# Seven weight buffers at seven offsets modulo 256 bytes, in an attention and two dense blocks on one core

## The chip, the core and the metric

One NeuronCore of a Trainium2 chip runs one program. The metric is device time in microseconds, the median of several executions. Engines are named as in the profile: PE (TensorE's matrix products), PEld (TensorE's loads of the stationary operand), DVE, ACT, POOL and SP, whose queue issues the transfers.

## What is computed

Attention over 2 x 8 heads of 768 tokens and width 64, with a mask (a query sees only the keys of the same 6-bit hash), and two dense blocks on the 1536 token rows of width 512:

```python
scores = np.where(q_bucket[..., None] == k_bucket[..., None, :], q @ k.T / 8, -1e9)
x = softmax(scores) @ v                                   # 1536 x 512 after the heads are joined
h = np.maximum(np.maximum(x @ w1, x @ w2), x @ w3)        # 512 -> 768
x = h @ w_out                                             # 768 -> 512
h = x @ w_in                                              # 512 -> 2048
g = np.where(h >= 1, h, np.where(h <= -1, 0, (h + 1) ** 2 / 4))
out = g @ w_out2                                          # 2048 -> 512
```

## The kernel before

Every float is kept as a high and a low part in a reduced format, and a product is made of three (high x high, high x low, low x high; `mm3`, L704 to L711), all summed in one PSUM bank.

**Attention** (L249 to L699) runs first. Its order on the engines comes from a planner (`Work`, L42 to L107) with costs and due times. PE makes the scores (`t_qk`, L374 and L377), transposes the exponentials against `ident` (`t_tr`, L404) and multiplies them by the values (`g_pv`, L422); `bits_mm` (L337) makes the hash bits. The sums of the exponentials of two heads lie in a tile `sums` (L393).

**The dense layers** (`mlp`, L713 to L862) follow, each matrix product 128 rows by 512 columns (L708 or L835), with a load of its own for the stationary operand. Layer 1 (`l1`) runs over 18 slices of the weights and three blocks of 512 tokens, 12 products each: stationary is the weight slice, moving is `x_hl`. Six pieces of it are made ahead, in part at half width. Layer 2 (L786 to L799) has the weights stationary and `hh` moving. Layer 3 (`l3`) has the weights stationary and `x_hl` moving. Layer 4 (`l4`, L824) has it reversed: `g` is stationary and the weights move. From its third unit on, layer 3 alternates with layer 4 by groups of 12 products.

**The weights** come in 58 slices. `w_load` fetches one, `w_steps` (L182 to L215) decodes it in six steps on ACT and DVE, the last of which is a cast of the high part into its buffer (L213), and `w_low` (L217) makes the low part on POOL. Slice n goes to buffer n mod 7: five buffers `w` in the pool `w_p`, and two buffers `wx` in a pool that is opened when attention's tiles are gone. Slices are decoded ahead of their use, in ticks between the products.

**Where the tiles lie.** Pools are laid out one behind the other in each partition. The offset of a tile modulo 256 bytes, in the built programs:

| tile | role | before | after the change |
|---|---|---|---|
| `ident`, `x_hl`, `wr`, `wg`, `wg2` | identity; activations; decoding | 0 | 0 |
| `w`, five buffers | weights | 0 each | 0, 32, 64, 96, 128 |
| `wx`, two buffers | weights | 128 each | 160, 192 |
| `hh`, `acc`, `g`, the dense layers' `r` | layer 2's input; sums; layer 4's input | 128 | 224 |
| `h0` to `h2` | layer 1's maxima | 0 | 160 |
| `hi`, `lo`, `qa`, `qb`, `p`, `pt`, `vr`, attention's `r`, `u` and more | attention | 128 | 160 |
| `pj_st`, high and low | hash projection | 64 and 240 | 64 and 240 |

Inside these tiles, products start at multiples of 256 bytes: the parts and blocks of a weight buffer lie 2048 and 512 bytes apart. A seventh of the slices, then, falls on each buffer.

Of the kernel before, what the change touches and what calls it, by code (L numbers as in the profile page):

```python
# [8 lines left out]
F32 = mybir.dt.float32  # L9
F32R = mybir.dt.float32r  # L10
# [9 lines left out]
NK = S // 128  # L20
# [90 lines left out]
def lsh_attention_moe_kernel(  # L111
# [21 lines left out]
    w_p = ctx.enter_context(tc.tile_pool(name="w", bufs=1))  # L133
    t_p = ctx.enter_context(tc.tile_pool(name="t", bufs=1))
    nm_p = ctx.enter_context(tc.tile_pool(name="nm", bufs=2))
# [30 lines left out]
        slices += s3[:1] + s4 + s3[1:]  # L166
    key_index = {key: n for n, (key, _, _) in enumerate(slices)}
    NSL = len(slices)
    WEARLY, WBUFS = 5, 7
    raws, splits, low_todo = {}, {}, []  # L170
    w_state = {"raw": 0, "done": 0, "base": 0, "gen": None, "auto": False, "more": None}

    def w_load(upto):
        while w_state["raw"] < min(upto, NSL):
            n = w_state["raw"]
            _, src, cols = slices[n]
            r = w_p.tile([128, 512, 2], I32, tag="wr", name="wr", bufs=2)
            nc.sync.dma_start(out=r[:, 0:cols, :].rearrange("p c t -> p (c t)"), in_=src.bitcast(I32))
            raws[n] = r
            w_state["raw"] += 1  # L180

    def w_steps(n):  # L182
        w_load(n + 2)
        cols = slices[n][2]
        r = raws.pop(n)
        low, high = r[:, 0:cols, 0], r[:, 0:cols, 1]
        g = w_p.tile([128, 512], I32, tag="wg", name="wg", bufs=2)[:, 0:cols]
        if w_state["auto"]:
            w_low()
        nc.scalar.activation(out=f32(g), in_=f32(high), func=ACTF.Square)  # L190
        yield
        nc.vector.scalar_tensor_tensor(  # L192
            out=f32(g), in0=f32(g), scalar=TINY_SQ, in1=f32(high), op0=ALU.is_ge, op1=ALU.mult
        )
        yield
        g2 = w_p.tile([128, 512], I32, tag="wg2", name="wg2", bufs=2)[:, 0:cols]
        nc.vector.tensor_scalar(  # L197
            out=g2, in0=g, scalar1=3, scalar2=0x3FFFFFF8, op0=ALU.logical_shift_left, op1=ALU.bitwise_and
        )
        yield  # L200
        nc.vector.scalar_tensor_tensor(
            out=g2, in0=g, scalar=-0x40000000, in1=g2, op0=ALU.bitwise_and, op1=ALU.bitwise_or
        )
        yield
        nc.vector.scalar_tensor_tensor(  # L205
            out=g2, in0=low, scalar=29, in1=g2, op0=ALU.logical_shift_right, op1=ALU.bitwise_or
        )
        yield
        if n % WBUFS < WEARLY:
            w = w_p.tile([128, 2, 512], F32R, tag="w", name="w", bufs=WEARLY)  # L210
        else:
            w = w_state["more"].tile([128, 2, 512], F32R, tag="wx", name="wx", bufs=WBUFS - WEARLY)
        nc.scalar.copy(out=w[:, 0, 0:cols], in_=f32(g2))  # L213
        splits[n] = w
        low_todo.append((n, w, g2, cols))  # L215

    def w_low():  # L217
        for n, w, g2, cols in low_todo:
            nc.gpsimd.tensor_tensor(out=w[:, 1, 0:cols], in0=f32(g2), in1=f32(w[:, 0, 0:cols]), op=ALU.subtract)  # L219
        low_todo.clear()  # L220

    def w_tick(count=1):
        for _ in range(count):
            if w_state["gen"] is None:
                n = w_state["done"]
                if n >= NSL:
                    w_low()
                if n >= NSL or n >= w_state["base"] + (WBUFS if w_state["more"] else WEARLY):
                    return
                w_state["gen"] = w_steps(n)  # L230
            try:
                next(w_state["gen"])
            except StopIteration:
                w_state["gen"] = None
                w_state["done"] += 1
# [13 lines left out]
    def attention(mlp_steps):  # L249
        with ExitStack() as ax, ExitStack() as sx:  # L250
# [10 lines left out]
            head, pair, tl, grp = {}, {}, {}, {}  # L261
# [128 lines left out]
            def t_exp(n):  # L390
                h, t = divmod(n, NK)
                if n % (2 * NK) == 0:
                    pair[h // 2] = dict(sums=nm_p.tile([128, 2 * NK], F32, tag="sums", name="sums"))  # L393
                p = tl[n]["p"]
                c = (h % 2) * NK + t
                nc.scalar.activation(  # L396
                    out=p, in_=p, func=ACTF.Exp, scale=-1.0, bias=tl[n]["nm"],
                    accum_out=pair[h // 2]["sums"][:, c:c + 1],
                )
# [199 lines left out]
            def tile_tasks(n):  # L599
                h, t = divmod(n, NK)  # L600
                g, r = divmod(n, 3)
                sp, pp = place("s", 1), place("p", 2)
                tb = [place(f"t{i}", 1) for i in range(2)]
                if n % (2 * NK) == 0:
                    sums_p[h // 2] = place("sums", 1)
                if r == 0:
                    pt_p_[g] = place("pt", 1)
                qk = task("PE", 0.75, n, t_qk, n, after=ready[h], takes=[sp], leaves=[h_place[h]])
                mx = task("DVE", 0.97, n, t_max, n, after=[qk], takes=[pp], leaves=[sp])
                ex = task("ACT", 1.06, n, t_exp, n, after=[mx], takes=[sums_p[h // 2]] if n % (2 * NK) == 0 else [], lag=0.1)  # L610
                exps[n] = ex
                outs, tr = [], None
                for half in range(2):
                    tr = task("PE", 0.325, n - 4, t_tr, n, half, after=[ex, tr], takes=[tb[half]], leaves=[pp], lag=0.1)
                    cp = task("ACT", 0.48, n - 2, t_out, n, half, nc.scalar.copy, after=[tr], takes=[pt_p_[g]] if r == 0 and half == 0 else [], leaves=[tb[half]])
                    work.also("DVE", 0.55, lambda a=(n, half, nc.vector.tensor_copy): t_out(*a), cp)
                    outs += [cp]
                return outs
# [34 lines left out]
            for n in range(NT_):  # L653
                h, t = divmod(n, NK)
# [259 lines left out]
```

## Time and profile before

| | us |
|---|---|
| median of 3 runs (704.96 to 705.01) | 704.96 |
| profiled execution | 704.98 |
| its span, first to last instruction | 703.2 |
| PE busy (99% of the span) | 695.2 |
| DVE, ACT, POOL busy | 455.5, 374.0, 282.7 |
| PE waiting for another engine, in all | under 5 |

The profiled execution's own time is 1.78 us over its span. A timeline's row gives a group's start and its length; the length reaches to the end of the last product, which is pipelined with the next group, so that the pace of a group is the difference of two starts over the count.

### The profile page before, as it was taken

The numbers are of one execution on the slowest core, as the hardware profiler recorded it, in microseconds if no ns is written. First come the engines' busy times: TensorE is split into PE (matmuls) and PEld (weight loads), VectorE is DVE, ScalarE is ACT, GpSimd is POOL, SyncE is SP. The second block draws the span as 40 slices with busy tenths as digits, with TensorE's granted clock in tenths as the row PEclk, the third lists the DMA queues.
The fourth block names the chain that finished last, engine by engine and source line by source line (L and its number), as shares of the span: only waits on it lengthen the run. The fifth ranks groups of instructions, "written<-read, shape, count | busy, mean of one in ns | idle before, by whom it ended". The sixth has DMA issues, their size and how long they took to land.

```text
span 703.2 us, 9982 instructions
## 1 busy us (share of the span) xinstructions
PE 695.2 (99%) x3548; PEld 553.9 (79%) x3548; DVE 455.5 (65%) x696; ACT 374.0 (53%) x733; POOL 282.7 (40%) x262
## 2 busy tenths in 40 slices
PE   8999999999999999999999999999999999999998
PEld 6777777777777688888888888888888888888886
DVE  6646555666655486775444355765888888888844
ACT  4788898888888423332321233665544444444430
POOL 3555646647523034442332022444344344344330
PEclk9999999999999999999999999999999999999999
DMA  5655557546511222221111022120111122111004
GB/s 164 162 149 151 132 145 202 139 121 167 132 46 45 95 91 90 90 91 52 56 49 54 31 89 90 47 75 31 60 61 61 60 66 84 61 61 60 31 0 180
DMA packets 25658, 62.78 MB, mean 89 GB/s; under 512 B 4085, under 2 KB 9813, under 8 KB 25609
## 3 DMA queue, kind: packets, MB, share of 16 engines
q1 hardware_dynamic: 25576, 62.15, 29.2%
q8 instruction: 28, 0.46, 0.3%
q14 instruction: 22, 0.17, 0.1%
q0 software_dynamic: 32, 0.00, 0.0%
HBM read 42.07 MB, written 3.19 MB: 64 GB/s over the span
## 4 chain that ended last, share of the span: by engine, by line
PE 97%; DVE 1%; issue 0%; DMA 0%; ACT 0%; DVEq 0%; ACTq 0%
PE b L708 47%; PE b L835 19%; PE u_ps L422 10%; PE t_ps L404 9%; PE s_ps L374 5%; PE s_ps L377 5%; PE pj_ps L337 2%; DMA r<-in_kq 0%; DVE p L384 0%; DVE lo L302 0%; DVE qb L344 0%; DVE qa L331 0%; DVE pt L413 0%; PE pj_ps L469 0%; ACT pt L413 0%
## 5 line engine op out<-in xcount | busy, mean ns | idle before, releaser
L708 PE MATMUL b<-x_hl,w 128*128 128x512 f32 (+1 forms) x900 | 203.1, 382 | 0.0
L708 PEld LDWEIGHTS b<-x_hl,w 128*128 128x128 f32 x900 | 164.0, 188 | 34.2 <-issue 0.6
L384 DVE TENSOR_SCALAR_CACHE_REDUCE p<-s_ps 128x768 f32<-128x768 f32 x96 | 91.1, 955 | 43.7 <-PE s_ps L377 32.4
L735 POOL TENSOR_TENSOR g<-r,g 128x512 fp32r<-128x512 f32 x48 | 62.6, 1306 | 125.6 <-ACT g L734 125.6
L835 PE MATMUL b<-w,g 128*128 128x512 f32 (+1 forms) x438 | 108.4, 392 | 0.0
L219 POOL TENSOR_TENSOR w<-wg,w 128x512 fp32r<-128x512 f32 (+1 forms) x42 | 59.4, 1414 | 96.7 <-ACT w L213 80.8
L835 PEld LDWEIGHTS b<-w,g 128*128 128x128 f32 x438 | 81.9, 189 | 18.7
L396 ACT ACTIVATE p<-p,nm 128x768 f32<-128x768 f32 x96 | 89.8, 937 | 9.0 <-DVE p L384 8.5
L192 DVE SCALAR_TENSOR_TENSOR wg<-wg,wr 128x512 f32<-128x512 f32 (+1 forms) x58 | 66.1, 1140 | 36.2 <-ACT wg L190 35.4
L213 ACT CAST w<-wg 128x512 fp32r<-128x512 f32 (+1 forms) x42 | 25.4, 605 | 115.6 <-DVE wg L205 115.6
L708 PE MATMUL b<-x_hl,wx 128*128 128x512 f32 x360 | 86.1, 395 | 0.0
L404 PEld LDWEIGHTS t_ps<-ident,p 128*128 128x128 f32 x576 | 66.5, 140 | 22.7 <-ACT p L396 11.5
L404 PE MATMUL t_ps<-ident,p 128*128 128x128 f32 x576 | 82.1, 276 | 1.1 <-DVE pt L413 0.9
L708 PEld LDWEIGHTS b<-x_hl,wx 128*128 128x128 f32 x360 | 67.9, 189 | 15.8
L413 ACT COPY pt<-t_ps 128x384 f32<-128x384 f32 x158 | 69.5, 480 | 18.2 <-PE t_ps L404 16.3
L374 PE MATMUL s_ps<-lo,qa 128*128 128x384 f32 x192 | 72.3, 377 | 1.0 <-DVE p L384 0.9
L422 PE MATMUL u_ps<-pt,vr 128*64 128x384 f32 x384 | 69.6, 495 | 0.2 <-ACT pt L413 0.2
L377 PE MATMUL s_ps<-hi,qb 76*128 76x384 f32 x192 | 65.3, 340 | 0.2 <-DVE hi L331 0.2
L815 DVE SCALAR_TENSOR_TENSOR r<-r,b 128x512 f32<-128x512 f32 x48 | 33.0, 687 | 48.2 <-ACT r L814 47.8
L842 DVE TENSOR_TENSOR acc<-b,acc 128x512 f32<-128x512 f32 (+1 forms) x85 | 56.5, 676 | 8.0 <-PE b L835 8.0
L813 ACT ACTIVATE r<-b,half_sb 128x512 f32<-128x512 f32 x48 | 32.9, 686 | 46.1 <-PE b L708 40.8
L197 DVE TENSOR_SCALAR wg<-wg 128x512 int32<-128x512 int32 (+1 forms) x58 | 53.9, 929 | 2.8
(80 smaller groups left out, 847.5 us busy)
## 6 DMA issues: line engine op xcount, KB each, us to landing
wr<-in_w SPq DMA_DIRECT2D x50, 512.0 KB, 3.1
r<-in_kq SPq DMA_DIRECT2D x15, 384.0 KB, 3.9
vr<-in_v SPq DMA_DIRECT2D x16, 192.0 KB
rb<-d SPq DMA_DIRECT2D x16, 192.0 KB, 3.3
wr<-in_w SPq DMA_DIRECT2D x8, 384.0 KB, 2.8
qa<-hi SPq DMA_DIRECT2D x15, 192.0 KB
qb<-hi SPq DMA_DIRECT2D x15, 192.0 KB, 4.0
qa<-lo SPq DMA_DIRECT2D x15, 192.0 KB, 2.7
```

Source lines behind the costliest of these rows:

```text
L192: nc.vector.scalar_tensor_tensor(out=f32(g), in0=f32(g), scalar=TINY_SQ, in1=f32(high), op0=ALU.is_ge, op1=ALU.mult)
L219: nc.gpsimd.tensor_tensor(out=w[:, 1, 0:cols], in0=f32(g2), in1=f32(w[:, 0, 0:cols]), op=ALU.subtract)
L374: nc.tensor.matmul(out=o, lhsT=hd["qa"][:, qs], rhs=hd["lo"][:, ks], start=True, stop=False)
L377: nc.tensor.matmul(out=o, lhsT=hd["qb"][0:76, qs], rhs=hd["hi"][0:76, ks], start=False, stop=True)
L384: nc.vector.tensor_scalar(out=p.rearrange("p (a k) -> p a k", a=2), in0=s_ps[n % 2][:, :, 0:HALF], scalar1=MASKED, scalar2=MASKED, op0=ALU ...
L396: nc.scalar.activation(out=p, in_=p, func=ACTF.Exp, scale=-1.0, bias=tl[n]["nm"], accum_out=pair[h // 2]["sums"][:, c:c + 1],)
L404: nc.tensor.transpose(out=t_ps[half][:, j * 128:(j + 1) * 128], in_=tl[n]["p"][:, kt * 128:(kt + 1) * 128], identity=ident,)
L413: copy(out=grp[g][:, 3 * half:3 * half + 3, r * 128:(r + 1) * 128], in_=t_ps[half][:, 0:HALF].rearrange("p (j q) -> p j q", j=3),)
L422: nc.tensor.matmul(out=u_ps[rows, 0:HALF], lhsT=vr[:, kt, :], rhs=grp[g][:, kt, :], start=(i == 0), stop=(i == 2),)
L708: nc.tensor.matmul(out=outp, lhsT=w_[a], rhs=x_[b_], start=(i == 0 and jj == 0), stop=(i == n - 1 and jj == 2),)
L735: nc.gpsimd.tensor_tensor(out=dst[:, 1, cs], in0=src, in1=f32(dst[:, 0, cs]), op=ALU.subtract)
L835: nc.tensor.matmul(out=pb[:, cs], lhsT=gs[f][:, a, tsl], rhs=wt[:, b_, cs], start=(n == 0), stop=(n == len(terms) - 1),)
```

## The change

The weight tiles are 8 elements (32 bytes) longer per partition, and the part in use is cut from the front of each. In one pool the buffers thereby begin 4128 bytes apart in place of 4096. `sums` is padded from 48 to 256 bytes, of which the first 48 are used. All tiles behind the weights move. The instructions, their number and their order on every engine are the same; addresses alone differ.

```diff
-    WEARLY, WBUFS = 5, 7
+    WEARLY, WBUFS, STAG = 5, 7, 8
...
         if n % WBUFS < WEARLY:
-            w = w_p.tile([128, 2, 512], F32R, tag="w", name="w", bufs=WEARLY)
+            w = w_p.tile([128, 2 * 512 + STAG], F32R, tag="w", name="w", bufs=WEARLY)
         else:
-            w = w_state["more"].tile([128, 2, 512], F32R, tag="wx", name="wx", bufs=WBUFS - WEARLY)
+            w = w_state["more"].tile([128, 2 * 512 + STAG], F32R, tag="wx", name="wx", bufs=WBUFS - WEARLY)
+        w = w[:, 0:2 * 512].rearrange("p (a c) -> p a c", a=2)
         nc.scalar.copy(out=w[:, 0, 0:cols], in_=f32(g2))
...
                 if n % (2 * NK) == 0:
-                    pair[h // 2] = dict(sums=nm_p.tile([128, 2 * NK], F32, tag="sums", name="sums"))
+                    pair[h // 2] = dict(sums=nm_p.tile([128, 64], F32, tag="sums", name="sums")[:, 0:2 * NK])
```

## Rows read from the trace of the kernel before

**Rows 1.** The page: span, busy time by engine, granted clock in 40 slices.

```profile
span 703.2 us, 9982 instructions
...
PE 695.2 (99%) x3548; PEld 553.9 (79%) x3548; DVE 455.5 (65%) x696; ACT 374.0 (53%) x733; POOL 282.7 (40%) x262
...
PEclk9999999999999999999999999999999999999999
```

**Rows 2.** The waits of PE: releaser, us in total, times, longest.

```profile
PE t_ps L265 <- DVE warm L147: 1.1, 1, 1.1
...
PE s_ps L377 <- DVE hi L331: 0.2, 1, 0.2
```

**Rows 3.** Groups of PE's products by line and shape; moving operand first, then stationary.

```profile
L708 PE MATMUL b<-x_hl,w 128*128 128x512 f32 x828 | 195.3, 391 | 0.0
L835 PE MATMUL b<-w,g 128*128 128x512 f32 x426 | 107.0, 395 | 0.0
L708 PE MATMUL b<-x_hl,wx 128*128 128x512 f32 x360 | 86.1, 395 | 0.0
L404 PE MATMUL t_ps<-ident,p 128*128 128x128 f32 x576 | 82.1, 276 | 1.1 <-DVE pt L413 0.9 <-ACT pt L413 0.2
...
L708 PE MATMUL b<-hh,w 128*128 128x512 f32 x162 | 38.7, 395 | 0.0
L835 PE MATMUL b<-wx,g 128*128 128x512 f32 x144 | 37.9, 391 | 0.0
...
L337 PE MATMUL pj_ps<-hi,pj_st 128*108 128x384 f32 x62 | 17.1, 355 | 1.1 <-ACT pj_st L289 0.6 <-DVE pj_st L290 0.5
L708 PE MATMUL b<-hh,wx 128*128 128x512 f32 x54 | 13.2, 392 | 0.0
L337 PE MATMUL pj_ps<-lo,pj_st 128*108 128x384 f32 x31 | 10.4, 337 | 0.0
```

**Rows 4.** PE's timeline, layer 1: start us, length us, line, operands, count.

```profile
293.19 41.02 PE L708 MATMUL b<-x_hl,w 128*128 128x512 f32 x180
334.05 16.91 PE L708 MATMUL b<-x_hl,wx 128*128 128x512 f32 x72
350.80 32.85 PE L708 MATMUL b<-x_hl,w 128*128 128x512 f32 x144
383.48 2.25 PE L708 MATMUL b<-hh,w 128*128 128x512 f32 x9
```

**Rows 5.** PE's timeline, layer 2 and the start of layer 3.

```profile
404.31 2.21 PE L708 MATMUL b<-hh,wx 128*128 128x512 f32 x9
406.36 27.36 PE L708 MATMUL b<-hh,w 128*128 128x512 f32 x117
433.55 16.89 PE L708 MATMUL b<-x_hl,wx 128*128 128x512 f32 x72
```

**Rows 6.** PE's timeline, layers 3 and 4 in turn, at two places.

```profile
453.01 2.96 PE L835 MATMUL b<-w,g 128*128 128x512 f32 x12
455.81 2.92 PE L708 MATMUL b<-x_hl,w 128*128 128x512 f32 x12
458.57 2.96 PE L835 MATMUL b<-w,g 128*128 128x512 f32 x12
...
486.33 2.89 PE L835 MATMUL b<-wx,g 128*128 128x512 f32 x12
489.06 2.89 PE L708 MATMUL b<-x_hl,w 128*128 128x512 f32 x12
491.79 2.89 PE L835 MATMUL b<-wx,g 128*128 128x512 f32 x12
```

**Rows 7.** The chain that ended last, layers 3 and 4, first and last piece.

```profile
453.18 2.80 PE b L835 x12
...
680.32 19.55 PE b L835 x90
```

**Rows 8.** POOL's group that writes the low parts into `w`: busy us, mean ns.

```profile
L219 POOL TENSOR_TENSOR w<-wg,w 128x512 fp32r<-128x512 f32 x36 | 53.3, 1480 | 67.7 <-ACT w L213 58.1 <-issue 9.4
```

## Prediction

> **What bounds the kernel now.** I read the page's busy shares first. TensorE is busy for 695.2 of 703.2 us, no other engine for more than 455.5 [rows 1], and its granted clock reads 9, nine tenths or more, in all 40 slices [rows 1]: the upper of its two levels, 2.4 GHz. The list of what PE waited for names eight waits, from 1.1 us down to 0.2 [rows 2]. So the time is PE's own pace, and faster or slower work of ACT, DVE and POOL reaches the end only when PE would wait for it.
>
> Then the pace of the products of the dense layers, in PE's timeline, as the start of one group less the start of the one before it, divided by its count. All are 128 rows by 512 columns with a weight load each, 1974 of them (828 + 426 + 360 + 162 + 144 + 54) [rows 3]. The reader is to see that they have **two paces**, and what separates them:
> - Layer 1, stationary operand in `w` (offset 0), moving `x_hl` (offset 0): 293.19 to 334.05 holds 180, so 227.0 ns each; 350.80 to 383.48 holds 144, 226.9 ns [rows 4].
> - Layer 1, stationary in `wx` (offset 128), moving `x_hl` (0): 334.05 to 350.80 holds 72, 232.6 ns [rows 4]; four slices of the 18 are in `wx`.
> - Layer 2 has it the other way round: moving `hh` lies at 128. Stationary in `w` (0): 406.36 to 433.55 holds 117, 232.4 ns. Stationary in `wx` (128): 404.31 to 406.36 holds 9, 227.8 ns [rows 5].
> - Layers 3 and 4 alternate in twelves. Where `g` (128) multiplies `w` (0), a twelve takes 2.80 us and the layer 3 twelve after it, though both its operands lie at 0, takes 2.76 (453.01, 455.81, 458.57). Where `g` (128) multiplies `wx` (128), both kinds take 2.73 (486.33, 489.06, 491.79) [rows 6].
>
> So PE runs at 226.9 ns where the two operands have the same offset modulo 256, and at 232.4 where they are 128 apart, in either direction; one unequal group also costs its equal neighbour some 2.5 ns each. The engine, the line and the clock are the same, and PE waits for nobody there. The steady difference of 5.5 ns is 2.4% of the pace. This is what the change turns.
>
> **The change part by part.** The instructions and their order stay. What moves is addresses (the table of offsets above).
>
> *The dense layers.* After the change the stationary operand of layers 1 and 3 stands 0, 32, 64, 96, 128, 160 or 192 bytes ahead of `x_hl`, each in a seventh of the slices. Layer 2 (`hh` at 224) and layer 4 (`g` at 224) get 32 to 224 and never 0. The trace has only the distances 0 and 128 for these products, so the price of the six new ones is open. The sum now, by stages:
> - layer 1: 612 full products, 144 of them from `wx`: 468 x 227.0 + 144 x 232.6 ns = 139.7 us [rows 4];
> - layer 2: 383.48 to 433.55 = 50.1 us for 216 [rows 4, 5];
> - the first 84 of layer 3: 433.55 to 453.01 = 19.5 us [rows 5, 6];
> - the rest: 453.18 to 699.87 (680.32 + 19.55) [rows 7], 246.7 us, less 1.4 for twelve half-width ones (116 ns each, half the slow pace), 245.3 us for 1062.
>
> Together 454.6 us for 1974, 230.3 ns on average. So today's kernel is already nearer the slow pace: most of layers 2 to 4 is unequal. After the change a seventh of layers 1 and 3, 170 products (612 + 576 over 7), keeps distance 0: 38.6 us at 227.0. The other 1804 break even at (454.6 - 38.6) / 1804 = **230.6 ns**. Every ns off that is worth 1.80 us.
>
> What pace do they get? Bounds from both sides: 232.4 ns (all like 128) gives 1804 x 1.8 ns = +3.2 us; 226.9 (all like 0) gives -6.7 us. That a new distance is better than 0, or worse than 128, nothing in the trace excludes; one step of 5.5 ns beyond either (221.4, 237.9) would give -16.6 and +13.2 us, which I keep as the outer ends with little weight. I take the middle of the two measured paces, 229.7 ns, as the distances 32 to 224 lie on a circle on which 0 and 128 are opposite, three to each side: 1804 x (229.7 - 230.6) = **-1.6 us**. By stage, layer 1 loses (468 products leave 227.0 for an average near 229.3, 139.7 to 140.3 us, +0.6), layer 2 gains (216 x 229.7 = 49.6, -0.5), the 1146 of layers 3 and 4 gain (264.8 to some 263.1, -1.7).
>
> *Attention.* `p`, `hi`, `lo`, `qa`, `qb`, `pt` and `vr` all shift by the same 32 bytes, so `s_ps` and `u_ps` keep their distances. Two pairs change: the transposes (`p` against `ident`, 128 to 160, 576 of them) and the bit products (`pj_st` against `hi` and `lo`, 93) [rows 3]. The trace has each at its present distance alone, with no second pace to change to. I take both at nothing; the bounds are a whole step of 5.5 ns each way, 576 x 5.5 = 3.2 us and 93 x 5.5 = 0.5 us.
>
> *The other engines.* ACT's casts and POOL's subtractions (36 of 1480 ns into `w` [rows 8]) write to new offsets. In the dense layers PE sits idle for 0.0 us before its products [rows 3], and the eight waits of the whole run, under 5 us together [rows 2], lie before them; that slack covers them. If the cover were gone, POOL's step would be late first, by a few per cent of its 1480 ns. The padded sums cost 384 bytes a partition and no instruction.
>
> **Rule and row.** The rows show PE slowed by where its two own operands stand. The Trainium skill says otherwise: "TensorE: Matmul & The Clock Gate", Part 2, gives PE two independent read ports and holds that loading the next weights takes no read bandwidth from the running matmul, and "SBUF — State Buffer", who interferes with whom, that PE waits on nobody. By that rule the sum is 0 and the time 705.0; the trace speaks against it with 227.0 against 232.4 ns.
>
> **The rivals.**
> 1. *No net change* (703.6 to 706.4). Either losses in layer 1 meet gains in layers 2 to 4 (new distances at 229.8 to 231.4 on average), or the pace doesn't hang on the distance at all but on something that goes along with it here, such as which tile is read: 705.0. The skill's rule above is the second of these. For the first: break-even lies inside the two measured paces. Against the second: `w` is fast with `x_hl` and slow with `hh`, and `wx` the reverse [rows 4, 5].
> 2. *Slower, the equal pace is lost.* If 226.9 belongs to equal offsets alone and every other distance runs like 128, 1804 products take 232.4: +3.2 us, **708.2**. It decides where the mean of the new distances passes 231.4. For it: in layers 3 and 4 even equal twelves slow to 2.76 us beside unequal ones [rows 6], and after the change nearly every twelve has unequal neighbours. Against it: two distances don't make a rule for eight.
> 3. *Most new distances are as good as 0.* If only those near 128 are slow, the mean is near 228: 1804 x -2.6 = -4.7 us, **700.3**. For it: layers 2 to 4 are where the slow pace sits now. Against it: the same twelves beside unequal ones.
>
> **How the numbers follow.** The profiled execution took 704.98 us, 1.78 us around its span, 0.02 over the median 704.96 of the runs; 704.98 - 1.6 = **703.4 us**. About 0.2% (1.4 us) is what a measurement can tell from none; the new distances must average under 229.85 ns for a gain that shows. Chances: forecast (702 to 703.55) 0.28, rival 3 and better 0.15, so faster 0.43; rival 1 0.32 (0.25 balance, 0.07 no dependence); rival 2 and worse 0.25. The range from 700.0 (mean 227.9 ns) to 708.2 (mean 232.4) leaves out the outer ends and a slow change in the transposes, some 2 in 10.
>
> **What would show it.** In the profile after: TensorE's share and the waits as now; in layer 1's timeline runs of 36 products per weight buffer with up to seven paces in turn, the fifth (distance 128) at 232.4 and the first at 227.0; no stretch of 180 at 227.0 left; layers 3 and 4 in twelves of 2.72 to 2.80 without the long 2.80/2.76 series. Attention should end within 1 us of 234.9. The prediction is wrong if layer 1 lies at 232 throughout (rival 2), if the paces don't differ by buffer (no dependence), if a buffer runs over 233 or under 226, or if the transposes' pace moves.

## The result and the profile after

The change takes 708.57 us (median of 3 runs, 708.56 to 708.71) against 704.96 before: ratio 1.0052, 95% interval 1.0034 to 1.007. It is slower by 3.6 us, about half a per cent, where a gain of 1.6 us was forecast; the range ended at 708.2.

The page after, its span and PE's busy time, in answer to [rows 1]:

```profile
span 706.9 us, 9982 instructions
...
PE 699.1 (99%) x3548; PEld 553.5 (78%) x3548; DVE 454.8 (64%) x696; ACT 374.3 (53%) x733; POOL 283.0 (40%) x262
```

The span grew by 3.7 us and PE's busy time by 3.9, with the same 3548 products; the other engines' busy times moved by 0.7 us at most. PE has the same eight waits as the list behind [rows 2], one of them 0.2 us shorter. So the time is again in the pace of PE.

Layer 1 of the changed kernel by slice. Each stretch runs from the first product of a slice to that of the next and holds 36 starts (the count of 37 includes one product that reaches in from before); columns: the stretch, its length, PE busy and count, granted clock, the DMA engines' share and GB/s. In the built program the five `w` buffers are handed out in the order 0, 128, 96, 64, 32, the first and then the others from the back. So from top to bottom the stationary operand stands 0, 128, 96, 64, 32, 160 and 192 bytes ahead of `x_hl`:

```profile
294.00:302.19 8.19, 8.19 (x37) 1.00 0.29 105
302.19:310.56 8.37, 8.37 (x37) 1.00 0.20 71
310.56:318.98 8.42, 8.42 (x37) 1.00 0.19 62
318.98:327.38 8.40, 8.40 (x37) 1.00 0.20 62
327.38:335.78 8.40, 8.40 (x37) 1.00 0.16 47
335.78:344.18 8.40, 8.40 (x37) 1.00 0.17 49
344.18:352.43 8.25, 8.25 (x37) 1.00 0.15 48
```

Read it as a length over 36 products: 227.5 ns at distance 0, then 232.5 at 128, 233.9 at 96, 233.3 at 64, 233.3 at 32, 233.3 at 160 and 229.2 at 192. One distance of seven is about as fast as before. Five lie at the slow pace of before (232.4 ns in [rows 5], 232.6 in [rows 4]) or over it, one between. The clock is 1.00 in every line, so it is none of it. The sum of the seven is 58.43 us; the same seven slices took 57.61 before (293.19 to 350.80, [rows 4]).

PE's timeline at the borders of the stages, in answer to [rows 4] and [rows 5]:

```profile
385.81 2.27 PE L709 MATMUL b<-hh,w 128*128 128x512 f32 x9
...
436.08 16.82 PE L709 MATMUL b<-x_hl,wx 128*128 128x512 f32 x72
...
455.49 0.85 PE L836 MATMUL b<-w,g 128*128 128x512 f32 x3
```

And the chain that ended last, pieces of layers 3 and 4 and the last one, in answer to [rows 6] and [rows 7]:

```profile
235.15 220.50 PE b L709 x984
...
455.65 2.77 PE b L836 x12
458.42 2.74 PE b L709 x12
...
469.45 2.79 PE b L709 x12
472.25 2.79 PE b L836 x12
...
684.07 19.55 PE b L836 x90
```

In [rows 6] a twelve of layer 4 took 2.80 us and one of layer 3 2.76, or both 2.73. Now both kinds wander between 2.74 and 2.80, and most lie at 2.77 or over. By stages, with the kernel before taken from [rows 4 to 7] and the first long piece of its own chain:

```profile
234.89 218.28 PE b L708 x984
```

The last column is the first run of the next section (the padding alone, all dense tiles at 0), also less the kernel before.

| stage | before | change | difference | all tiles at 0 |
|---|---|---|---|---|
| attention, to the first product of layer 1 | 234.89 | 235.15 | +0.26 | +0.27 |
| layer 1 | 148.59 | 150.66 | +2.07 | -0.89 |
| layer 2 | 50.07 | 50.27 | +0.20 | -1.11 |
| layer 3 before layer 4 sets in | 19.46 | 19.41 | -0.05 | -0.42 |
| layers 3 and 4 | 246.69 | 247.97 | +1.28 | -4.53 |

The differences of the change sum to 3.76 us, those of the run at 0 to -6.68; the spans moved by 3.7 and -6.7.

### The profile page after: what moved, and what is told of

The parts are those of the page before. It is cut to its first block, busy times and chain, and to the rows that moved or that the text cites. A ratio compares the mean times of both kernels' runs of the same rounds, so it can differ in the third digit from the quotient of the medians.

```text
span 706.9 us, 9982 instructions
## 1 busy us (share of the span) xinstructions
PE 699.1 (99%) x3548; PEld 553.5 (78%) x3548; DVE 454.8 (64%) x696; ACT 374.3 (53%) x733; POOL 283.0 (40%) x262
## 4 chain that ended last, share of the span: by engine, by line
PE 97%; DVE 1%; issue 0%; DMA 0%; ACT 0%; DVEq 0%; ACTq 0%
PE b L709 47%; PE b L836 19%; PE u_ps L423 10%; PE t_ps L405 9%; PE s_ps L375 5%; PE s_ps L378 5%; PE pj_ps L338 2%; DMA r<-in_kq 0%; DVE p L385 0%; DVE lo L303 0%; DVE qb L345 0%; DVE qa L332 0%; DVE pt L414 0%; PE pj_ps L470 0%; ACT pt L414 0%
## 5 line engine op out<-in xcount | busy, mean ns | idle before, releaser
L709 PE MATMUL b<-x_hl,w 128*128 128x512 f32 (+1 forms) x900 | 206.4, 385 | 0.0
```

The source lines that it names most:

```text
L709: nc.tensor.matmul(out=outp, lhsT=w_[a], rhs=x_[b_], start=(i == 0 and jj == 0), stop=(i == n - 1 and jj == 2),)
```

## The experiments

**The padding alone.** The kernel before, and of the change only the padded `sums`. Its 256-byte tiles put everything behind the weights on 0 modulo 256: `wx`, `hh` and `g` as well as `w` and `x_hl`, and attention's tiles too.

```diff
-    ... sums=nm_p.tile([128, 2 * NK], F32, tag="sums", name="sums")
+    ... sums=nm_p.tile([128, 64], F32, tag="sums", name="sums")[:, 0:2 * NK]
```

> The kernel before with the sums padded to 256 bytes and no stagger: every dense tile (w, wx, x_hl, hh, g) then begins at the same offset modulo 256, 0. Theory A (PE's pace hangs on the distance of its two operands modulo 256, and only distance 0 gives the fast pace): all 1974 dense products at 227.0 ns in place of 230.3 on average, 454.6 to 448.1 us, so 698.5 us, and no stretch of 232 in layers 2 to 4. Rival B (weight buffers that share an offset slow each other, as one is written while another is read): nothing gained, 705 us, or up to 709 if wx now shares with w. Rival C (the change's loss came from moving the tiles behind the weights, by the padding): slower than 705, near 708.5.

Measured: 698.15 us against 705.02 for the kernel before on the same chip, ratio 0.9902 (0.9887 to 0.9917). The chain that ended last in this run:

```profile
235.16 215.86 PE b L708 x984
451.02 2.72 PE b L835 x12
453.75 2.72 PE b L708 x12
456.46 2.72 PE b L835 x12
674.06 19.12 PE b L835 x90
```

Its timeline, layers 1 and 2 and what follows:

```profile
276.78 16.48 PE L708 MATMUL b<-x_hl,wx 128*128 128x512 f32 x72
293.10 40.96 PE L708 MATMUL b<-x_hl,w 128*128 128x512 f32 x180
333.90 16.48 PE L708 MATMUL b<-x_hl,wx 128*128 128x512 f32 x72
...
382.86 2.20 PE L708 MATMUL b<-hh,w 128*128 128x512 f32 x9
...
405.30 26.68 PE L708 MATMUL b<-hh,w 128*128 128x512 f32 x117
431.82 16.48 PE L708 MATMUL b<-x_hl,wx 128*128 128x512 f32 x72
448.14 2.88 PE L708 MATMUL b<-x_hl,w 128*128 128x512 f32 x12
450.86 2.88 PE L835 MATMUL b<-w,g 128*128 128x512 f32 x12
```

`wx` with `x_hl` is as fast as `w` now (293.10 - 276.78 over 72 and 333.90 - 293.10 over 180 are both 226.7 ns), `hh` with `w` too (431.82 - 405.30 over 117 = 226.7), and the twelves of layers 3 and 4 take 2.72 us each (226.7 ns a product), with nothing lost where the two layers meet. Theory A holds to 0.4 us. Rival B falls: all seven buffers share one offset here while ACT and POOL write some and PE reads others. Rival C falls too: the same padding that the change has is worth -6.9 us when the stagger is left out. Attention didn't gain: `p` now stands at the offset of `ident`, and within their groups the transposes start 116.7 ns apart on average, as in the traces of before (distance 128), of the change (160) and of the next run (32). So what follows is shown for the dense products, not for the transposes.

**The stagger alone.**

```diff
 (the change)
-    ... sums=nm_p.tile([128, 64], F32, tag="sums", name="sums")[:, 0:2 * NK]
+    ... sums=nm_p.tile([128, 2 * NK], F32, tag="sums", name="sums")
```

> The stagger alone, sums not padded: w at 0, 32, 64, 96, 128 as in the change, wx at 32 and 64, hh and g at 96. Theory A: nearly every distance is unequal still, so the change's time, 708.6 us within 1, with the five w buffers of layer 1 at the paces of the change (229.2, 232.4, 234.6, 233.3, 233.3 ns) and the two wx buffers now like the second and third w buffer (232.4, 234.6) in place of 233.4 and 229.2; layer 2 fast only in slices whose buffer lies at 96. Rival C (padding is to blame): 705 us.

Measured: 709.24 us, ratio 1.0059 (1.0044 to 1.0074). The two `wx` buffers, now 32 and 64 bytes ahead, in layer 1 (columns as above):

```profile
335.94:344.34 8.40, 8.40 (x37) 1.00 0.17 49
344.34:352.74 8.40, 8.40 (x37) 1.00 0.16 47
```

That is 233.3 ns each, which is what the buffers at 32 and 64 took in the change (its fifth and fourth stretch above), and the five `w` buffers run as in the change (227.2 to 233.9 ns by the starts in the trace), so theory A holds here too. The 232.4 and 234.6 of the expectation came from taking the buffers in the order of their offsets, in which they are not handed out; the stretches at the second and third place are those at 128 and 96. The seventh buffer is slower than in the change (it was 229.2 at 192). In layer 2 the buffer at 96, the offset of `hh`, is the fastest as expected, but takes 229.4 ns beside unequal products (27 starts in the trace; the other four distances 232.1 to 233.7). The total is as expected. So the loss is the stagger's: it costs 10.4 us on the padded kernel (698.15 to 708.57) and 4.2 on the kernel before (705.02 to 709.24). The padding is worth 6.9 us without the stagger and 0.7 with it (709.24 to 708.57), as most distances are then unequal either way.

**One common place that is not 0.**

```diff
 (the padding alone)
-    warm = const.tile([128, CH], BF16, name="warm")
+    warm = const.tile([128, CH + 32], BF16, name="warm")[:, 0:CH]
```

> As the first run, with every tile from the identity on 64 bytes further, so that all operands of the dense products begin at 64 modulo 256. Theory A (distance alone counts): the time of the first run within 0.3 us, 698.5 us by the theory. Rival D (the place itself counts, tiles must begin at a multiple of 256 or 128): slower than the first run, up to 708 us if all products take 232.

Measured: 698.28 us, ratio 0.9903 (0.9887 to 0.992). From its chain:

```profile
235.19 215.82 PE b L708 x984
451.01 2.72 PE b L835 x12
```

The twelves take 2.72 us as in the first run. A common place at 64 costs no more than one at 0; the distance has a price.

**A stagger of 256 bytes.**

```diff
 (the change)
-    WEARLY, WBUFS, STAG = 5, 7, 8
+    WEARLY, WBUFS, STAG = 5, 7, 64
```

> The change with a stagger of 256 bytes in place of 32: every buffer begins at 0 modulo 256, but at 0, 256, 0, 256, 0 and so on modulo 512. Theory A with a period of 256 bytes: the time of the first run within 0.3 us, 698.5 us by the theory. If the period is 512 or more: three of seven buffers at some 232 ns, about 2.5 us per 460 products, 701 to 703 us. Rival B (buffers must not share an offset): 705 us or more.

Measured: 698.16 us, ratio 0.9902 (0.9887 to 0.9917). Seven different places whose distances are multiples of 256 cost nothing: 256 bytes is a period of it.

**Steps of 4 bytes.**

```diff
 (the stagger of 256 bytes)
-        w = w[:, 0:2 * 512].rearrange("p (a c) -> p a c", a=2)
+        s = n % WBUFS
+        w = w[:, s:s + 2 * 512].rearrange("p (a c) -> p a c", a=2)
```

> Every dense tile at 0 modulo 256 as in the first run, but the seven weight buffers are used from 0, 4, 8, 12, 16, 20 and 24 bytes on (each buffer 4352 bytes long). Theory A1 (the two operands must begin in the same 32 bytes of the 256): the first run's 698.2 us. Theory A2 (the same byte is needed): six of seven buffers at 231 to 235 ns as with the distances of 32 and more, 707 to 709 us. Theory A3 (the loss grows with the distance): layer 1 by buffer 226.7 ns at 0 and up step by step, about 701 us.

Measured: 708.07 us, ratio 1.0048 (1.0031 to 1.0064). Layer 1 by slice, from distance 0 to 24 (columns as above):

```profile
293.62:301.79 8.17, 8.17 (x37) 1.00 0.23 80
301.79:310.16 8.37, 8.37 (x37) 1.00 0.18 65
310.16:318.45 8.30, 8.30 (x37) 1.00 0.20 63
318.45:326.75 8.29, 8.29 (x37) 1.00 0.18 63
326.75:335.14 8.39, 8.39 (x37) 1.00 0.14 47
335.14:343.54 8.40, 8.40 (x37) 1.00 0.16 49
343.54:351.86 8.32, 8.32 (x37) 1.00 0.16 47
```

Over 36: 226.9 ns at 0, then 232.5 at 4 bytes, 230.5, 230.3, 233.1, 233.3 and 231.1. One element of distance costs nearly as much as 32 bytes (233.3 ns above). A1 (the same 32 bytes) falls, and so does A3, as the loss does not grow with the distance; A2 holds in its time and in four of the six buffers, the two at 230.5 and 230.3 lie just under its 231.

**Just below 256.**

```diff
 (the run before)
-        s = n % WBUFS
+        s = (0, 60, 56, 48, 52, 4, 8)[n % WBUFS]
```

> As the run before, with the seven buffers used from 0, 240, 224, 192, 208, 16 and 32 bytes modulo 256: the distances that the change has not, just below 256, with 192 and 32 once more. Theory A2: every buffer but the first at 231 to 235 ns, 707 to 709 us. Theory A1 or A3, read on both sides: 240 and 16 near 227, 32 at 232.4 and 192 at 229.2 ns in layer 1 as in the change, 224 between; 703 to 706 us. A pace under 226.7 in any buffer would mean that distance 0 is not the best.

Measured: 707.17 us, ratio 1.0033 (1.002 to 1.0046). Layer 1 by slice, distances 0, 240, 224, 192, 208, 16, 32:

```profile
293.67:301.86 8.18, 8.18 (x37) 1.00 0.29 93
301.86:310.02 8.17, 8.17 (x37) 1.00 0.25 82
310.02:318.42 8.39, 8.39 (x37) 1.00 0.18 62
318.42:326.66 8.24, 8.24 (x37) 1.00 0.18 64
326.66:335.01 8.36, 8.36 (x37) 1.00 0.12 47
335.01:343.42 8.40, 8.40 (x37) 1.00 0.15 49
343.42:351.81 8.40, 8.40 (x37) 1.00 0.16 47
```

Here 240 is as fast as 0 (8.17 us over 36, 226.9 ns), against A2; 224 (233.1), 208 (232.1) and 16 (233.3) are slow, 192 has its 229 and 32 its 233 again. So equal offsets are not the only fast pair, but 13 of the 15 unequal distances that layer 1 meets in these runs and the change cost from 3.4 to 7 ns each; 240 costs nothing and 192 some 2. None runs under 226.7.

Among unequal products a fast pair loses its pace. In layer 4 of the run with steps of 4 bytes, two buffers alternate by three products; there the single starts in the trace give 232.5 ns at distance 0 (105 products) and 232.6 at 240 (72), in the midst of the other distances (230.0 to 235.7).

**The hash projection at the same place.**

```diff
 (the padding alone)
-    pj_raw = const.tile([128, 108], F32, name="pj_raw")
-    pj_st = const.tile([128, 2, 108], F32R, name="pj_st")
+    pj_raw = const.tile([128, 160], F32, name="pj_raw")[:, 0:108]
+    pj_st = const.tile([128, 2, 128], F32R, name="pj_st")[:, :, 0:108]
...
-    warm = const.tile([128, CH], BF16, name="warm")
+    warm = const.tile([128, CH + 80], BF16, name="warm")[:, 0:CH]
```

> The first run with the hash projection's two parts moved from 64 and 240 to 0 modulo 256, the offset of hi and lo, so that attention's bit products have distance 0 too; identity and x_hl stay at 0. Theory A, if short products gain as the long ones: 93 products by up to 5 ns, 0.3 to 0.5 us less than the first run, 697.7 us. If runs of two or three products among others are too short to reach the fast pace: no change within 0.2 us.

Measured: 698.08 us, ratio 0.9903 (0.9888 to 0.9918), 0.07 us from the first run, which ran on another chip. No change: the 93 short products come in twos and threes and gain nothing that can be told.

**Which pair: a product's own, or the next load?** The stationary operand of a product is loaded while the product before it streams (in the trace of before, the load for a product of layers 2 to 4 begins 1 to 4 ns after the start of the product before and takes 188), so the distance could count in a product or across two.

```diff
 (the padding alone)
-    x_hl = x_p.tile([128, 2, 4, NT], F32R, name="x_hl")
+    x_hl = x_p.tile([128, 2, 4 * NT + 32], F32R, name="x_hl")[:, :, 0:4 * NT].rearrange("p a (k t) -> p a k t", k=4)
...
-    w = w_p.tile([128, 2, 512], F32R, tag="w", name="w", bufs=WEARLY)
+    w = w_p.tile([128, 2, 512 + 32], F32R, tag="w", name="w", bufs=WEARLY)
...
-    hh["t"] = h_p.tile([128, 6, 2, NT], F32R, name="hh")
+    hh["t"] = h_p.tile([128, 6, 2, NT + 32], F32R, name="hh")
...
-    gt = g_p.tile([128, 2, NT], F32R, tag="g", name="g", bufs=4)
+    gt = g_p.tile([128, 2, NT + 32], F32R, tag="g", name="g", bufs=4)
```

(`wx` as `w`.)

> The first run with the low parts (of w, wx, x_hl, hh and g) 128 bytes further than the high parts, which stay at 0. In a triple (high x high, high x low, low x high) the two operands of one product are then 128 apart in the second and the third product; but the stationary operand that is loaded for the NEXT product always has the offset of the moving operand of the product that runs (0 and 0, 128 and 128, 0 and 0). Theory N (the load ahead meets the running stream, so the next product's stationary counts): no unequal pair, near the first run, 226.7 to 229 ns, 698.2 to 702 us. Theory O (a product's own two operands count): two of three products unequal, 230.5 to 232.5 ns, 705.5 to 709.5 us.

Measured: 706.63 us, ratio 1.0025 (1.0015 to 1.0035). In its timeline `x_hl` with `wx` and with `w` take the same:

```profile
277.01 16.80 PE L708 MATMUL b<-x_hl,wx 128*128 128x512 f32 x72
293.65 41.76 PE L708 MATMUL b<-x_hl,w 128*128 128x512 f32 x180
```

That is 16.64 us over 72, 231.1 ns, or 693.3 ns for a triple in place of 680.0. The number lies where theory O put it, but the run doesn't prove it: the place of the streams changes twice in every triple, and such a change has a price even where each product's own pair is equal. [Rows 6] show that: beside `wx` all products of both layers had equal operands, layer 3 at 0 and layer 4 at 128, and a twelve took 2.73 us; here above, with one place for all, 2.72. The single starts in the trace show that these 10 ns fall on the border: the last product of such a twelve takes 233 ns and the first of the next 230, those in between 226 or 227. Theory N alone, without such a price, falls. Which of the two pairs counts stays open.

## Why the prediction was wrong

*What bounds the kernel, and the two paces*: right. PE's pace is the whole of it, the other engines' cover held, and the two paces of the dense products hang on the distance of PE's two operands, as the runs at one common place show (698.15 and 698.28 us).

*The table by stages and the break-even of 230.6 ns*: right as arithmetic. With 170 products kept at 227.0 and the others at a mean of 230.6, nothing would have moved. But the equal products did not keep 227.0. Their starts in the trace after give 228.9 ns (167 products), those of layer 3 among them 229.9 (72): +0.3 us. The prediction had seen the reason, the price that an equal group pays beside an unequal one, and left it out of this term. The trace of before shows where it is paid: in the 16 equal twelves of layer 3 between unequal ones of layer 4, the first seven products take 231.0 ns on average, the next four 226.8, the last 232.5.

*"I take the middle of the two measured paces, 229.7 ns, as the distances 32 to 224 lie on a circle"*: this is the step that failed. It mis-sized the one open term. The six unequal stretches of layer 1 above average 232.6 ns ((8.37 + 8.42 + 8.40 + 8.40 + 8.40 + 8.25) us / 216); over all stages the starts in the trace give 232.4 (1805 products). 1804 x (232.4 - 230.6) ns is +3.2 us, where 229.7 gave -1.6; with the 0.3 us of the equal products and the 0.26 of attention that is the loss, to within 0.2 us. The pace is no smooth function between two opposite points: it jumps at the first 4 bytes, and 232 is not the slow end but the usual level. 0 was not one point of eight; it was a special one.

*By stage*: layer 1 was to lose 0.6 us and lost 2.07. Layer 2 was to gain 0.5 and lost 0.20; layers 3 and 4 were to gain 1.7 and lost 1.23 (+1.28 - 0.05). Their slow twelves had nothing to lose, but nothing to gain either, and the fast ones of [rows 6] went.

*Rival 2, the equal pace is lost, at 708.2 us with a chance of 0.25*: this is what happened, with the place and the sign as written. Its pace of 232.4 is the mean that came: four distances run slower (32, 64, 96 and 160 at 233.3 to 233.9), layer 1's 192 runs faster (229.2). It came out 0.4 us short, as the equal products and attention lost those 0.3 and 0.26 us. The range ended on this rival's own number, so that everything worse, which the prediction counted in the same 0.25, lay outside it. The argument held against it, that two distances make no rule for eight, was fair; the same holds for the middle between them.

*Rival 3* had one case in the change, 192 at 229.2; 240, which the change does not have, is a second. *Rival 1*: the paces differ by buffer under one line of code, so there is dependence, and no balance.

*Attention at nothing*: the transposes' pace did not move. Attention ended 0.26 us later, inside the bounds. The padding alone (235.16 us) and the stagger alone (235.20) show the same shift; nothing here settles where it arises.

*What would show it*: distance 128 was to run at 232.4 and did (232.5), as the second stretch and not the fifth. A buffer over 233, named as a sign of being wrong, came four times.

*The rule against the row.* The Trainium skill's Part 2 of "TensorE: Matmul & The Clock Gate" has the load of the next weights take nothing from the running product. By it neither the change nor the padding would do anything. The trace disagrees in both directions: 708.57 us against 704.96, and 698.15 against 705.02, with only addresses changed. What in the chip makes the addresses count, no run here shows.

## What to carry to other kernels

Where PE is the bound and its long products come back to back, list the addresses of both its operands modulo 256, in the order in which the built program hands the buffers out, and read the pace (start to start over the count) by pair of tiles. Giving all matrix operands one common offset, by padding whatever small tile stands ahead of them, was worth 1% here and cost 384 bytes a partition; spreading them cost half a per cent. A few equal pairs among unequal ones gain little. And where a trace has only two points of an unknown curve, the better one may be special: test it by making everything equal before making everything different.

## What the runs showed of the hardware that I had not expected

With one common offset the products take 226.7 ns in every steady stretch, at 0 and at 64 alike, with distances of 256 free. A distance of one element (4 bytes) costs 5.6 ns of 227, about as much as one of 32 bytes (5.8) or 128 (5.0); 96 bytes cost 6.4 over the same kernel's distance 0. In layer 1's runs of 36 a stationary operand 16 bytes behind the moving one (240) is as fast as an equal one, 16 bytes ahead it is not (233.3 ns). The transposes keep 116.7 ns at distances 0, 32, 128 and 160. Why, the profile doesn't show.
